# Two attentions in one kernel: output sums added by VectorE alone, and a softmax over eight places cut into short steps

## The chip, the cores and the metric

One Trainium2 chip, one core of it. The metric is the device time of one launch in microseconds (us). Engines are called by the names of the profile: PE (TensorE), with PEld for its weight loads, DVE (VectorE), ACT (ScalarE), POOL (GpSimd), SP (SyncE, which issues nearly all DMAs). Each engine runs its own instructions in order and waits on semaphores for the others.

## The reference

Two attention layers, A and B, on separate inputs of shape 1 x 2048 x 576, with 32 heads of 18 each; their outputs stand side by side. B is plain softmax attention. A looks at eight places only, two positions apart:

```python
W, dil = 8, 2
idx = pos[:, None] - (jnp.arange(W) * dil)[None, :]
mask = idx >= 0
logits = jnp.einsum("bhsd,bhswd->bhsw", q, kg) * scale      # kg, vg: k and v at idx
logits = jnp.where(mask, logits, -1e9)
attn = _softmax(logits, axis=-1)
o = jnp.einsum("bhsw,bhswd->bhsd", attn, vg)
return o.transpose(...).reshape(B, S, D) @ wo
```

## The kernel before, in words

Everything is float32, products split into high and low parts. A first part, up to about 420 us, makes the projections of both layers. Then comes the main loop of 512 steps, which is written out by hand: the program says for every engine in which order it works.

One step is one tile of 128 keys for one block of 512 queries and a group of four heads of B. PE makes four score matmuls (`score`, line 227), each into a bank of the ring "scores" (four PSUM banks); ACT takes the exponential of each (line 233). Beside three or four of the scores PE makes a matmul for the row maxima of a later block (line 162) into the ring "else" (three banks), and DVE reduces each to its maximum (line 169). At the end of the step the exponentials of the step before are weighed with the values (`weigh`, line 700, into the bank `po`).

All other work hangs in an agenda: a function due at step n is called at the end of step n (`due()`), and so stands in the program at that place. The order on each engine follows from that, while an engine may run its instructions earlier than the step, as far as what they wait for allows. Functions due at the same step are called in the order in which they were entered; `later(n, f)` enters f n steps ahead.

- A's attention runs in eight rounds, `local(j)`, j = 0 to 7, one each 54 steps; round j counts its plan from step 10 + 54 j. POOL makes the logits out of nine products (`match`, lines 823 and 827; the sum `lg`, line 830). DVE takes the maximum over the eight places (`most`, line 837, tile `am`), POOL subtracts it (`lower`, 844), ACT takes the exponentials (847), DVE sums them and takes the reciprocal (`total`, 837 and 851, tile `as`), POOL multiplies (`share`, 854) and then makes nine weighted terms (`weighted`, 860 to 863). `upper` and `rest` (867, 872) split the result, `put` and `get` (875, 885, 887) carry it through DRAM into another order. All POOL work of a round takes most of the round's time.
- A's output products, four in each round (two tiles of 128 positions, two halves of 288 columns), are put inside a step between two scores (`sums_of_a`): PE sums the two halves of the contraction in two banks, `one` (of the ring "scores") and `two` (of the ring "else"), beside each other (`beside`, line 979). ACT copies `one`, DVE copies `two` to SBUF, and POOL adds them (line 906).
- When a block of B is done, `finish` copies `po` out and, by `later`, at +7 takes reciprocals of the denominators (731), at +8 and +12 carries them through DRAM to all rows (732, 733), and at +17, +18, +19 POOL scales and splits the result (734, 735, 736). A block ends every 16 steps, so line 734 falls due at steps 33, 49, ..., 193, 209, ...
- The weights of A's output product are loaded and split in five pieces (`load_wo`), due at steps 28, 32, 36, 40 and 44; POOL splits each three steps later (lines 107 and 108).
- `halve` splits the row maxima of B for their way back into the queries (107, 108).

Of the kernel before, what the change touches and what calls it, by code (L numbers as in the profile page):

```python
# [7 lines left out]
F32 = mybir.dt.float32  # L8
F32R = mybir.dt.float32r
BF16 = mybir.dt.bfloat16  # L10
AF = mybir.ActivationFunctionType
ALU = mybir.AluOpType
# [8 lines left out]
W = 8  # L21
# [27 lines left out]
def ap(t, *dims):  # L49

    return bass.AP(tensor=t.tensor, offset=t.offset, ap=[list(t.ap[0])] + [list(d) for d in dims])
# [8 lines left out]
def two_attentions(ctx: ExitStack, tc, xa, wa, woa, xb, wb, wob, c_id, c_sel, out):  # L60
# [56 lines left out]
    def plan(start, pieces):  # L117
        for n, f in pieces:
            agenda[start + n].append(f)
# [100 lines left out]
    def score(g, b, kt, h, also, kind="scores"):  # L220

        assert (g, b) in placed
        qs, ks = sets[g % 3]
        p, r = divmod(h, 2)
        ps = bank(kind)
        at = slice(64 * r, 64 * r + 56)
        nc.tensor.matmul(ps, ks[at, p, 128 * kt : 128 * kt + 128], qs[at, b, p], start=True, stop=True)  # L227
        reduce = maximum(1 - r) if also else None

        counted[0] += 1  # L230
        early = counted[0] % 8 < 6
        e = (e_room if early else work).tile([128, 512], F32, name="e", bufs=6 if early else 2)
        nc.scalar.activation(e, ps, AF.Exp, scale=SCALE)  # L233
        if reduce:
            reduce()
        return e
# [560 lines left out]
    def local(j):  # L797

        st = {}
        p0 = AB * j  # L800

        def arrange(n):
            wide = (HALO if n else 0) + SUB
            load(rows(dparts[j][n][0, 0], (wide, D), (D * wide, 4), (1, wide)),
                 rows(da[D * n, HALO + p0 + SUB - wide :], (HALO + S, D), (SUB, 4), (1, wide)))


        def fetch(nm):
            halo = 0 if nm == "q" else HALO
            n = DH * (halo + SUB)  # L810
            t = st[nm] = work.tile([128, DH, halo + SUB], F32, name="akv" if halo else "aq", bufs=2 if halo else 1)
            load(ap(t, (1, n)), rows(dparts[j]["qkv".index(nm)][0, 0], (n, 128), (1, n)))

        def window(t, c):

            return ap(t[:, 2 * c, HALO:], (HALO + SUB, 2), (-DIL, W), (1, SUB))

        def wide():
            return work.tile([128, 2, W, SUB], F32, name="pr", bufs=2)

        def match(c):
            pr = wide()
            nc.gpsimd.tensor_mul(pr, ap(st["q"][:, 2 * c], (SUB, 2), (0, W), (1, SUB)), window(st["k"], c))  # L823
            if c == 0:
                st["pr"] = pr
            else:
                nc.gpsimd.tensor_add(st["pr"], st["pr"], pr)  # L827
            if c == DH // 2 - 1:
                lg = st["lg"] = work.tile([128, W, SUB], F32, name="lg", bufs=1)
                nc.gpsimd.tensor_add(lg, st["pr"][:, 0], st["pr"][:, 1])  # L830
                if j == 0:
                    for w in range(1, W):
                        nc.gpsimd.memset(lg[:32, w, : DIL * w], MASKED)

        def over_window(op, name):
            t = work.tile([128, SUB], F32, name=name, bufs=1)
            nc.vector.tensor_reduce(t, st["lg"].rearrange("p w i -> p i w"), axis=AX.X, op=op)
            return t

        def most():  # L840
            st["m"] = over_window(ALU.max, "am")

        def lower():
            nc.gpsimd.tensor_sub(st["lg"], st["lg"], ap(st["m"], (0, W), (1, SUB)))

        def exponents():
            nc.scalar.activation(st["lg"], st["lg"], AF.Exp, scale=SCALE)

        def total():
            s = st["s"] = over_window(ALU.add, "as")  # L850
            nc.vector.reciprocal(s, s)

        def share():
            nc.gpsimd.tensor_mul(st["lg"], st["lg"], ap(st["s"], (0, W), (1, SUB)))

        def weighted(c):
            if c == 0:
                st["o"] = work.tile([128, DH, SUB], F32, name="ao", bufs=1)
            at = wide()
            nc.gpsimd.tensor_mul(at, ap(st["lg"], (0, 2), (SUB, W), (1, SUB)), window(st["v"], c))  # L860
            nc.gpsimd.tensor_add(at[:, :, :4], at[:, :, :4], at[:, :, 4:])  # L861
            nc.gpsimd.tensor_add(at[:, :, :2], at[:, :, :2], at[:, :, 2:4])
            nc.gpsimd.tensor_add(st["o"][:, 2 * c : 2 * c + 2], at[:, :, 0], at[:, :, 1])

        def upper():
            hi = work.tile([128, DH, SUB], F32R, name="aohi", bufs=1)
            nc.gpsimd.tensor_copy(hi, st["o"])
            st["parts"] = hi, st["o"].bitcast(F32R)

        def rest():  # L870
            hi, lo = st["parts"]
            nc.gpsimd.tensor_sub(lo, st["o"], hi)

        def put(i):
            load(rows(dao[j, i, 0, 0], (DH * SUB, 128), (1, DH * SUB)),
                 ap(st["parts"][i].bitcast(F32), (1, DH * SUB)))

        def get(n):
            st["x"] = []
            st["n"] = n  # L880
            last = work.tile([128, 128], F32R, name="ahl", bufs=1)
            for i in range(2):
                t = work.tile([128, 4, 128], F32R, name=f"at{i}", bufs=1)
                for s in range(2):
                    load(t.bitcast(F32)[:, :, SUB * s : SUB * s + SUB],
                         dao[j, i, 2 * n + s, :512].rearrange("(c p) n -> p c n", p=128))
                load(last.bitcast(F32)[64 * i : 64 * i + 64].rearrange("p (s n) -> p s n", s=2),
                     rows(dao[j, i, 2 * n, 512], (SUB, 64), (D * SUB, 2), (1, SUB)))
                st["x"].append([t[:, c] for c in range(4)])
            st["x"].append(last)  # L890

        def finished(h):
            inside.append(lambda: sums_of_a(h))

        def sums_of_a(h):
            his, los = zip(*wo["a"])
            w = his[:4], los[:4], his[4], los[4]
            cols = slice(288 * h, 288 * h + 288)
            if h == 0:
                st["y"] = ys["a", j, st["n"]] = work.tile([128, D], F32, name="y", bufs=3)  # L900
            one, two = beside("scores", *(halves(r, 0, w, st["x"], cols, slice(0, 128), True) for r in range(2)))
            y = st["y"][:, cols]
            part = work.tile([128, 288], F32, name="part", bufs=2)
            nc.scalar.activation(y, one, AF.Copy)
            nc.vector.tensor_copy(part, two)  # L905
            nc.gpsimd.tensor_add(y, y, part)  # L906

        plan = {0: lambda: fetch("q"), 1: lambda: fetch("k"), 28: lambda: fetch("v"), 29: most, 30: lower,
                32: exponents, 34: total, 35: share, 58: upper, 59: rest, 66: lambda: put(0), 67: lambda: put(1)}
        for c in range(DH // 2):  # L910
            plan[5 + 5 * c // 2] = lambda c=c: match(c)
            plan[36 + 5 * c // 2] = lambda c=c: weighted(c)
        for n in range(3):
            plan[(-24 if j else -7) + n] = lambda n=n: arrange(n)
        for n in range(2):
            at = 74 + 7 * n
            plan[at] = lambda n=n: get(n)
            plan[at + 4] = lambda: finished(0)
            plan[at + 6] = lambda: finished(1)
            producing.update((A_FROM + GAP * j + at + 5, A_FROM + GAP * j + at + 7))  # L920
            plan[at + 12] = lambda n=n: load(out[p0 + 128 * n : p0 + 128 * n + 128, :D], ys["a", j, n])
        return plan


    olds = defaultdict(list)
# [33 lines left out]


    inside = []

    waiting = []

# [92 lines left out]
    ):  # L1057
        plan(start, [(4 * c, lambda k=k, src=src, ch=ch: load_wo(k, src, *ch)) for c, ch in enumerate(chunks)])
    for j in range(NJ):
        plan(A_FROM + GAP * j, local(j).items())  # L1060
    for g in range(1, NG):
        if g > EARLY:
            plan(STEPS * (g - 2) + 1, [(n, f) for n, f in enumerate(stack_loads(g))])
# [35 lines left out]
    while step < ALL:  # L1099
        n, kt = divmod(step, NT)  # L1100
        g, b = divmod(n, NB)
        places = positions(min(4 if behind() > 0 else 3, total - sum(given)))
        es = []
        for h in range(4):

            if inside and h == (3 if 3 in places else 2):
                inside.pop(0)()
            es.append(score(g, b, kt, h, h in places))
        while waiting:
            waiting.pop(0)()  # L1110
        if ready:
            weigh(*ready.pop(0))
        ready.append((g, b, kt, es))
        due()
        if waiting:
            waiting.pop(0)()
        step += 1
# [30 lines left out]
```

## Time and profile before

| | |
|---|---|
| median of 3 runs | 1677.24 us (1673.43 to 1678.26) |
| the profiled execution, its own time | 1677.95 us |
| its span in the profile | 1676.2 us |
| mean granted PE clock | 0.998 |
| busy: PE, DVE, ACT, POOL | 1664.2, 1410.6, 1223.3, 998.6 us |

The span runs from the first instruction to the last; the execution's own time has 1.75 us more around it. Rows of a timeline give the start in us from the span's start, the duration, engine, line of the kernel, operation, result and operands, shapes and count, and in brackets the idle time of the engine before it, with what ended it. Rows of a group give, behind the shapes, the count, then total busy us, mean ns of one, and the idle time before them.

### The profile page before, as it was taken

Reading aid. Unit: us, or ns where it says so; the run is one execution under the profiler, and the core shown is the slowest. Engines: PE = TensorE matmul, PEld = TensorE weight load, DVE = VectorE, ACT = ScalarE, POOL = GpSimd, SP = SyncE. Lnnn points to the kernel's source line nnn. Section 1 sums busy time; section 2 is a strip of 40 time slices with the busy share of each in tenths; the row PEclk is TensorE's granted clock in tenths of the full one; section 3 lists DMA queues with packets and bytes.
Section 4 is the critical chain, followed back from the end, with each engine's and each line's share of the span. In section 5 each row is a group of like instructions: output and inputs, shape, how many; then the busy total and the mean of one; then the engine's idle time right before and its main releaser. Section 6 shows DMA issues by size and latency. Waiting matters only on the chain.

```text
span 1676.2 us, 33705 instructions
## 1 busy us (share of the span) xinstructions
PE 1664.2 (99%) x12994; PEld 922.9 (55%) x12994; DVE 1410.6 (84%) x2318; ACT 1223.3 (73%) x2420; POOL 998.6 (60%) x842
## 2 busy tenths in 40 slices
PE   9999999999999999999999999999999999999998
PEld 7998888887433444344444344444444344344765
DVE  5199999999889989889889988889888989888433
ACT  6423521211999988988988987998988988988444
POOL 2306732100286996986984996986995997812010
PEclk9999999999999999999999999999999999999999
DMA  8938944421624536165247128227526222134101
GB/s 246 242 108 220 264 141 135 139 90 66 94 82 62 142 99 107 59 155 115 66 107 156 64 84 181 70 63 134 132 64 131 76 76 77 35 98 170 57 30 58
DMA packets 186082, 188.37 MB, mean 112 GB/s; under 512 B 114832, under 2 KB 129936, under 8 KB 184192
## 3 DMA queue, kind: packets, MB, share of 16 engines
q1 hardware_dynamic: 181056, 174.66, 40.1%
q0 software_dynamic: 4032, 10.63, 3.1%
q8 instruction: 102, 1.67, 0.4%
q10 hardware_dynamic: 832, 0.92, 0.2%
q14 instruction: 60, 0.49, 0.1%
HBM read 113.30 MB, written 88.12 MB: 120 GB/s over the span
## 4 chain that ended last, share of the span: by engine, by line
PE 89%; POOL 6%; SPq 2%; DVE 1%; DMA 1%; issue 1%; ACT 0%; POOLq 0%; ACTq 0%; DVEq 0%
PE po L700 27%; PE bank L227 21%; PE bank L320 14%; PE bank L162 14%; PE bank L979 7%; PE bank L257 4%; SPq L146 1%; POOL pr L823 1%; POOL pr L860 1%; POOL pr L827 1%; DVE mx L169 1%; POOL pr L861 1%; DMA rec<-drec 1%; PE bank L958 1%; PE bank L181 0%
## 5 line engine op out<-in xcount | busy, mean ns | idle before, releaser
L169 DVE TENSOR_REDUCE mx<-bank 128x1 f32<-128x512 f32 x2048 | 1294.4, 685 | 154.1 <-PE bank L162 132.0
L233 ACT ACTIVATE e<-bank 128x512 f32<-128x512 f32 x2048 | 1060.4, 610 | 108.6 <-PE bank L227 57.1
L162 PE MATMUL bank<-ks,qs 54*128 54x512 f32 x2048 | 757.6, 424 | 5.0 <-DVE mx L169 2.7
L227 PE MATMUL bank<-qs,ks 56*128 56x512 f32 x2048 | 582.9, 425 | 0.0
L227 PEld LDWEIGHTS bank<-qs,ks 56*128 56x128 f32 x2048 | 327.2, 186 | 430.7 <-ACT e L233 403.1
L700 PE MATMUL po<-e,v 128*19 128x512 f32 x4096 | 541.0, 600 | 0.0
L162 PEld LDWEIGHTS bank<-ks,qs 54*128 54x128 f32 x2048 | 342.8, 185 | 34.2 <-DVE mx L169 16.8
L823 POOL TENSOR_TENSOR pr<-aq,akv 128x1024 f32<-128x1024 f32 x72 | 157.9, 2197 | 24.6 <-PE po L700 22.3
L700 PEld LDWEIGHTS po<-e,v 128*19 128x19 f32 x4096 | 69.8, 97 | 181.7 <-issue 170.7
L860 POOL TENSOR_TENSOR pr<-lg,akv 128x1024 f32<-128x1024 f32 x72 | 158.1, 2195 | 0.3
L827 POOL TENSOR_TENSOR pr<-pr 128x1024 f32<-128x1024 f32 x64 | 152.4, 2382 | 5.0
L651 ACT ACTIVATE ohi<-bank 128x512 f32<-128x512 f32 (+1 forms) x56 | 30.4, 595 | 155.2 <-issue 124.4
L320 PE MATMUL bank<-xlo,ahi 64*128 64x512 f32 (+1 forms) x448 | 121.8, 391 | 0.1
L320 PE MATMUL bank<-xhi,alo 64*128 64x512 f32 (+1 forms) x448 | 118.6, 390 | 0.0
L320 PE MATMUL bank<-xhi,ahi 64*128 64x512 f32 (+1 forms) x448 | 115.2, 392 | 0.0
L906 POOL TENSOR_TENSOR y<-y,part 128x288 f32<-128x288 f32 x32 | 25.6, 799 | 117.8 <-DVE part L905 102.4
L861 POOL TENSOR_TENSOR pr<-pr 128x512 f32<-128x512 f32 x72 | 92.4, 1283 | 5.6
L461 POOL TENSOR_TENSOR olo<-olo,ohi 128x512 fp32r<-128x512 f32 x36 | 46.2, 1298 | 68.3 <-ACT ohi L460 67.1
L368 POOL TENSOR_TENSOR alo<-raw,ahi 128x512 fp32r<-128x512 f32 (+1 forms) x14 | 17.6, 1254 | 115.1 <-ACT ahi L367 90.6
L320 PEld LDWEIGHTS bank<-xlo,ahi 64*128 64x128 f32 (+1 forms) x448 | 68.1, 182 | 9.4 <-POOL xlo L368 0.5
L320 PEld LDWEIGHTS bank<-xhi,alo 64*128 64x128 f32 (+1 forms) x448 | 65.4, 182 | 9.1
L979 PE MATMUL bank<-wohi,at 64*128 64x288 f32 x512 | 68.9, 301 | 0.0
(194 smaller groups left out, 1845.4 us busy)
## 6 DMA issues: line engine op xcount, KB each, us to landing
do<-n SPq DMA_DIRECT2D x28, 512.0 KB
da<-ohi SPq DMA_DIRECT2D x52, 256.0 KB
dpart<-da SPq DMA_DIRECT2D x16, 702.0 KB
akv<-dpart SPq DMA_DIRECT2D x16, 702.0 KB
out<-y SPq DMA_DIRECT2D x32, 288.0 KB
qs<-dqk SPq DMA_DIRECT2D x30, 288.0 KB
ks<-dqk SPq DMA_DIRECT2D x30, 288.0 KB
at<-dao SPq DMA_DIRECT2D x64, 128.0 KB
```

What stands on the lines that cost most here:

```text
L162: nc.tensor.matmul(ps, qs[at, b, p, 128 * t : 128 * t + 128], ks[at, p, 512 * k : 512 * k + 512], start=True, stop=True)
L169: nc.vector.tensor_reduce(mx[:, r, p, t, k : k + 1], ps, axis=AX.X, op=ALU.max)
L227: nc.tensor.matmul(ps, ks[at, p, 128 * kt : 128 * kt + 128], qs[at, b, p], start=True, stop=True)
L233: nc.scalar.activation(e, ps, AF.Exp, scale=SCALE)
L257: nc.tensor.matmul(ps, a, b, start=c == i == 0, stop=c == 4 and i == 1)
L320: nc.tensor.matmul(ps, a, b, start=start, stop=stop)
L700: nc.tensor.matmul(po[32 * i : 32 * i + 19], vs[g][:, kt, 19 * i : 19 * i + 19], es[i], start=kt == 0, stop=kt == NT - 1)
L823: nc.gpsimd.tensor_mul(pr, ap(st["q"][:, 2 * c], (SUB, 2), (0, W), (1, SUB)), window(st["k"], c))
L827: nc.gpsimd.tensor_add(st["pr"], st["pr"], pr)
L860: nc.gpsimd.tensor_mul(at, ap(st["lg"], (0, 2), (SUB, W), (1, SUB)), window(st["v"], c))
L861: nc.gpsimd.tensor_add(at[:, :, :4], at[:, :, :4], at[:, :, 4:])
L979: nc.tensor.matmul(ps, a, b, start=start, stop=stop)
```

## The change

In the output products ACT copies `two` to SBUF, and DVE adds `one` to it from PSUM, in place. That addition is not called at once but entered in a new list, `outside`, which is emptied after the step's four scores (and so after the reductions beside them); POOL's addition is gone.

In A's softmax the reduction over eight places becomes three tensor_tensor steps on DVE, halving the places each time (8 to 4, 4 to 2, 2 to 1), for the maxima and for the sums alike; the reciprocal is taken in two halves of 32 columns. In the round's plan `most` falls on steps 29, 30, 30 (was 29), `lower` on 31 (30), the exponentials on 33 (32), `total` on 35, 36, 36 (34), the two halves of the reciprocal on 36 and 37, `share` on 38 (35), the nine `weighted` from 39 on (36), `upper` on 61 (58), `rest` on 62 (59), `put` on 67 and 68 (66, 67). The matches, fetches, gets and output products keep their steps.

```diff
-        def over_window(op, name):
-            t = work.tile([128, SUB], F32, name=name, bufs=1)
-            nc.vector.tensor_reduce(t, st["lg"].rearrange("p w i -> p i w"), axis=AX.X, op=op)
-            return t
-
-        def most():
-            st["m"] = over_window(ALU.max, "am")
+        def over_window(op, name, n):
+
+            if n == 0:
+                st[name] = work.tile([128, W // 2, SUB], F32, name=name, bufs=1)
+            t, half = st[name], W >> n + 1
+            src = st["lg"] if n == 0 else t
+            nc.vector.tensor_tensor(t[:, :half], src[:, :half], src[:, half : 2 * half], op=op)
+
+        def most(n):
+            over_window(ALU.max, "am", n)
...
-        def total():
-            s = st["s"] = over_window(ALU.add, "as")
-            nc.vector.reciprocal(s, s)
+        def total(n):
+            over_window(ALU.add, "as", n)
+
+        def inverse(n):
+            half = st["as"][:, 0, SUB // 2 * n : SUB // 2 * n + SUB // 2]
+            nc.vector.reciprocal(half, half)
...
-            part = work.tile([128, 288], F32, name="part", bufs=2)
-            nc.scalar.activation(y, one, AF.Copy)
-            nc.vector.tensor_copy(part, two)
-            nc.gpsimd.tensor_add(y, y, part)
-
-        plan = {0: lambda: fetch("q"), 1: lambda: fetch("k"), 28: lambda: fetch("v"), 29: most, 30: lower,
-                32: exponents, 34: total, 35: share, 58: upper, 59: rest, 66: lambda: put(0), 67: lambda: put(1)}
+            nc.scalar.activation(y, two, AF.Copy)
+            outside.append(lambda: nc.vector.tensor_add(y, one, y))
+
+        plan = {0: lambda: fetch("q"), 1: lambda: fetch("k"), 28: lambda: fetch("v"), 31: lower,
+                33: exponents, 38: share, 61: upper, 62: rest, 67: lambda: put(0), 68: lambda: put(1)}
+
+        short = [(at, lambda f=f, n=n: f(n)) for f, ats in ((most, (29, 30, 30)), (total, (35, 36, 36)), (inverse, (36, 37)))
+                 for n, at in enumerate(ats)]
         for c in range(DH // 2):
             plan[5 + 5 * c // 2] = lambda c=c: match(c)
-            plan[36 + 5 * c // 2] = lambda c=c: weighted(c)
+            plan[39 + 5 * c // 2] = lambda c=c: weighted(c)
...
             es.append(score(g, b, kt, h, h in places))
+        while outside:
+            outside.pop(0)()
         while waiting:
```

More of the change, by code (lines that the diff above doesn't have):

```diff
@@ L833, in match @@
                         nc.gpsimd.memset(lg[:32, w, : DIL * w], MASKED)
-        def over_window(op, name):
-            t = work.tile([128, SUB], F32, name=name, bufs=1)
-            nc.vector.tensor_reduce(t, st["lg"].rearrange("p w i -> p i w"), axis=AX.X, op=op)
-            return t
-        def most():
-            st["m"] = over_window(ALU.max, "am")
+        def over_window(op, name, n):
[6 more added lines that the diff above has]
+            over_window(ALU.max, "am", n)
         def lower():
-            nc.gpsimd.tensor_sub(st["lg"], st["lg"], ap(st["m"], (0, W), (1, SUB)))
+            nc.gpsimd.tensor_sub(st["lg"], st["lg"], ap(st["am"], (0, W), (1, SUB)))
         def exponents():
             nc.scalar.activation(st["lg"], st["lg"], AF.Exp, scale=SCALE)
-        def total():
-            s = st["s"] = over_window(ALU.add, "as")
-            nc.vector.reciprocal(s, s)
+        def total(n):
[3 more added lines that the diff above has]
+            nc.vector.reciprocal(half, half)
         def share():
-            nc.gpsimd.tensor_mul(st["lg"], st["lg"], ap(st["s"], (0, W), (1, SUB)))
+            nc.gpsimd.tensor_mul(st["lg"], st["lg"], ap(st["as"], (0, W), (1, SUB)))
         def weighted(c):
@@ L921, in local @@
             plan[at + 12] = lambda n=n: load(out[p0 + 128 * n : p0 + 128 * n + 128, :D], ys["a", j, n])
-        return plan
+        return [*plan.items(), *short]
     olds = defaultdict(list)
@@ L961, in two_attentions @@
     inside = []
+    outside = []
     waiting = []
@@ L1059, in two_attentions @@
     for j in range(NJ):
-        plan(A_FROM + GAP * j, local(j).items())
+        plan(A_FROM + GAP * j, local(j))
     for g in range(1, NG):
```

## The prediction

> **What bounds the kernel now.** I read the page first, then the groups of instructions by line, the waits, the chain, and the timelines of single engines in a few windows.
>
> ```profile
> span 1676.2 us, 33705 instructions
> ...
> PE 1664.2 (99%) x12994; PEld 922.9 (55%) x12994; DVE 1410.6 (84%) x2318; ACT 1223.3 (73%) x2420; POOL 998.6 (60%) x842
> ```
>
> TensorE sets the time; only what keeps it waiting is worth anything. A step of the main loop (four score matmuls, three maximum matmuls, the weighing at line 700) begins each weighing one period after the last. Two stretches of TensorE's timeline, then VectorE's in a normal step:
>
> ```profile
> 1261.30 1.05 PE L700 MATMUL po<-e,v 128*19 128x512 f32 x8
> 1263.41 1.05 PE L700 MATMUL po<-e,v 128*19 128x512 f32 x8
> 1266.09 1.05 PE L700 MATMUL po<-e,v 128*19 128x512 f32 x8
> ...
> 1153.61 1.05 PE L700 MATMUL po<-e,v 128*19 128x512 f32 x8
> 1156.30 1.05 PE L700 MATMUL po<-e,v 128*19 128x512 f32 x8
> ```
>
> ```profile
> 1004.93 1.89 DVE L169 TENSOR_REDUCE mx<-bank 128x1 f32<-128x512 f32 x3 [0.23 <-PE bank L162]
> ```
>
> A normal period is 2.11 us (1263.41 - 1261.30). Two are long: 2.68 us, after round 6's maxima, and 2.69 us, after round 5's sums. In a step VectorE works 1.89 us and rests 0.23; a long operation between holds up its reductions, these hold three banks, and TensorE waits for a bank. That is what the split into short steps can remove: 0.57 us for the maxima, 0.58 for the sums, in each of eight rounds.
>
> There is a much dearer form of the same wait, once in the run, when VectorE stands at the maxima and GpSimd has not yet made the logits:
>
> ```profile
> 1009.66 1.03 DVE L837 TENSOR_REDUCE am<-lg 128x64 f32<-128x512 f32 x1 [2.84 <-POOL lg L830]
> ```
>
> ```profile
> 1007.62 1.05 PE L700 MATMUL po<-e,v 128*19 128x512 f32 x8
> ...
> 1011.35 0.79 PE L162 MATMUL bank<-ks,qs 54*128 54x512 f32 x1 [2.24 <-DVE mx L169]
> ...
> 1013.69 1.91 PE L700 MATMUL po<-e,v 128*19 128x512 f32 x8
> ```
>
> ```profile
> 1008.60:1017.20 8.60, 6.36 (x28) 3.32 (x26) 5.42 (x9) 4.08 (x8) 4.28 (x4) 0.63 1.12 145
> ```
>
> The last row is a table by stretch: its length, the busy time of each engine, then the granted clock. VectorE is blocked for 3.87 us (2.84 + 1.03). The period is 6.07 us (1013.69 - 1007.62), 3.96 over normal; and afterwards the granted clock is 0.63 over 8.6 us, weighing takes 1.91 instead of 1.05, so I put the whole loss at 5.7 us: the 1.7 is an estimate for the next, slowed period, between the 0.86 of its weighing and the 3.2 (8.6 x 0.37) of the whole window. [...]
>
> **The change, part by part.** The groups that carry the prices:
>
> ```profile
> L169 DVE TENSOR_REDUCE mx<-bank 128x1 f32<-128x512 f32 x2048 | 1294.4, 685 | 154.1 <-PE bank L162 132.0 <-PE bank L227 10.9 <-PE bank L320 1.1
> ...
> L906 POOL TENSOR_TENSOR y<-y,part 128x288 f32<-128x288 f32 x32 | 25.6, 799 | 117.8 <-DVE part L905 102.4 <-ACT y L904 13.1 <-ACT e L233 2.3
> ...
> L999 DVE TENSOR_TENSOR y<-bank,y 128x288 f32<-128x288 f32 x24 | 11.0, 458 | 2.5
> ...
> L837 DVE TENSOR_REDUCE as<-lg 128x64 f32<-128x512 f32 x8 | 8.5, 1062 | 0.0
> L837 DVE TENSOR_REDUCE am<-lg 128x64 f32<-128x512 f32 x8 | 8.4, 1054 | 2.8 <-POOL lg L830 2.8
> ...
> L731 DVE RECIPROCAL den<-den 128x16 f32<-128x16 f32 x29 | 7.0, 243 | 0.0
> ...
> L851 DVE RECIPROCAL as<-as 128x64 f32<-128x64 f32 x8 | 4.4, 553 | 0.3
> ```
>
> *Short steps.* No row shows tensor_tensor at these sizes. From 685 ns for 512 elements and 458 for 288 (1.01 ns an element, 0.17 fixed) I estimate 0.43 us for 256, 0.30 for 128 and 0.23 for 64; a half reciprocal, between 243 ns for 16 and 553 for 64, 0.35. Maxima: 0.43 in one step, 0.53 in the next, instead of 1.05 at once. Sums and reciprocal: 0.43, then 0.88 (0.30 + 0.23 + 0.35), then 0.35, instead of 1.62 (1.06 + 0.55). VectorE's work hardly shrinks; it is spread. What then remains of the 1.15 us a round? The maxima row says that 1.05 us in one place loses 0.57, so 0.48 is absorbed; by that measure 0.43 and 0.53 lose almost nothing in the maxima, but 0.88 loses about 0.4 and the 0.35 behind it 0.1 more, and if backlogs add up up to 1.1 us. The sums row says that 1.62 loses only 0.58, so 1.04 is absorbed, and nothing would remain. I take 0.4 a round, nearer to the sums row because the pieces concerned are its own. Removed: six maxima stalls of 0.57 (rounds 1 and 4 are treated below) and eight of 0.58, 8.1 us; left, 8 x 0.4 = 3.2. Sum -4.9 us.
>
> *Output products.* ScalarE copies the other bank, at the same place and price. VectorE's copy (0.45 us, first row below) becomes an addition (458 ns): the same, nothing. But it moves behind the step's last reduction and holds the bank of the scores ring that ScalarE used to free. The bank is wanted in the next step:
>
> ```profile
> 1250.41 0.45 DVE L905 COPY part<-bank 128x288 f32<-128x288 f32 x1
> 1250.78 0.68 DVE L169 TENSOR_REDUCE mx<-bank 128x1 f32<-128x512 f32 x1
> ```
>
> ```profile
> 1251.86 0.39 PE L227 MATMUL bank<-qs,ks 56*128 56x512 f32 x1
> ```
>
> Order swapped, the reduction ends at about 1251.1 and the addition at 1251.56, 0.3 us before the score matmul that reuses the bank. What is queued behind the addition is the next step's reductions, and they would have stood behind the copy too. Below: nothing is gained, since the maximum ring's bank, now freed earlier, is not what TensorE waits for. Above: one late VectorE operation of 0.2 us in each of 32, 6 us. I take one in eight, 0.8 us.
>
> GpSimd loses 32 x 0.8 = 25.6 us of work and 117.8 us of standing in order for it. None of this is on TensorE's path by itself; it counts only through the logits' readiness, next.
>
> *The shifted plan.* A's lower, exponents, share, weighted terms and puts move by 1, 1, 3, 3 and 1 steps. GpSimd works in order, so what matters is what now stands ahead of share. Finishing steps of B and weight splits fall due at fixed steps, and two of them wait for a DMA. Round 0: share moves from step 45 to 48, and the split of A's last weight piece is due at step 47:
>
> ```profile
> 521.35 1.28 POOL L854 TENSOR_TENSOR lg<-lg,as 128x512 f32<-128x512 f32 x1 [2.90 <-DVE as L851]
> ...
> 529.61 0.67 POOL L107 CAST wohi<-y 128x576 fp32r<-128x576 f32 x1 [2.00 <-DMA y<-woa]
> ...
> 531.73 2.21 POOL L860 TENSOR_TENSOR pr<-lg,akv 128x1024 f32<-128x1024 f32 x1
> ```
>
> Before, share and the first weighted term filled the time to 527.6 (529.61 - 2.00). Now GpSimd idles until the DMA lands at 529.5, splits, and does these 6.26 us (527.61 - 521.35) from 531.7 on. Behind that it is busy without a rest until round 1's logits:
>
> ```profile
> 626.11 1.28 POOL L830 TENSOR_TENSOR lg<-pr 128x512 f32<-128x512 f32 x1
> ```
>
> ```profile
> 629.51 1.05 DVE L837 TENSOR_REDUCE am<-lg 128x64 f32<-128x512 f32 x1
> ```
>
> They were ready at 627.39, 2.1 us before they were wanted. With +6.26 and one addition of 0.8 less they come at 632.85, 3.3 us late. VectorE is blocked 3.3 + 0.43 = 3.8 us, as long as in the stall shown above, so the same 5.7 us instead of 0.57: +5.1.
>
> Round 3: share moves from step 207 to 210, and the scaling of B's outputs (line 734), due at 209, now stands ahead of it. It waited for the DMA of the reciprocals, held up in the SP queue by loads of keys:
>
> ```profile
> 899.54 2.19 POOL L860 TENSOR_TENSOR pr<-lg,akv 128x1024 f32<-128x1024 f32 x1
> ...
> 903.98 0.46 POOL L863 TENSOR_TENSOR ao<-pr 128x128 f32<-128x128 f32 x1
> 914.08 1.29 POOL L734 TENSOR_TENSOR o<-o,rec 128x512 f32<-128x512 f32 x1 [9.64 <-DMA rec<-drec]
> ```
>
> Share (1.28, as in round 0) and the first term (903.98 + 0.46 - 899.54 = 4.9) move behind the 9.64 us wait: 6.2, less one addition, 5.4 us more for round 4's logits, which are the late ones. VectorE's first piece is 0.6 shorter: +4.7.
>
> The puts (one step later) wait on SP for upper and rest, which now stand behind one or two match products; SP is held a few us in rounds 0 and 3. Queued there are gets due six steps later, 12.7 us, which covers it; uncovered, the output products would wait for what is left of that hold.
>
> *The lock.* The new steps read two tensors of SBUF while GpSimd may be reading:
>
> ```profile
> 20.45 1.37 DVE L368 TENSOR_TENSOR xlo<-raw,xhi 128x512 fp32r<-128x512 f32 x1 [0.98 <-ACT xhi L367]
> ```
>
> ```profile
> 19.98 1.29 POOL L461 TENSOR_TENSOR olo<-olo,ohi 128x512 fp32r<-128x512 f32 x1 [19.04 <-ACT ohi L460]
> ```
>
> Such a VectorE step took 1.37 us and ended 0.55 after GpSimd's. In most rounds GpSimd waits for the very result, so it is idle; only finishing work of rounds 6 and 7 overlaps. Between 0 and 4 x 0.9 us I take 0.7. [...]
>
> **Sum**, against the profiled run's own 1677.95 us (0.7 above the median 1677.24): -4.9 + 0.8 + 5.1 + 4.7 + 0.7 = +6.4, so 1684.4 us.
>
> **Rivals.** (a) The two DMAs land earlier than in this one execution, or the stalls are absorbed: then -4.9 + 1.5 = -3.4, 1674.5, and with nothing left of the stalls (-8.1) 1671.3. For: both are single waits of 2.0 and 9.64 us. Against: GpSimd has no slack behind them. Chance 0.24. (b) Only one of the two comes late: 1679.5. Chance 0.17. (c) More rounds are late, share being 5 us later everywhere (three periods of 2.11, less 1.3 that one half reciprocal is shorter than reduction and reciprocal). The tightest is round 7, whose logits led by 2.5 us:
>
> ```profile
> 1384.39 1.28 POOL L830 TENSOR_TENSOR lg<-pr 128x512 f32<-128x512 f32 x1
> ```
>
> ```profile
> 1388.19 1.07 DVE L837 TENSOR_REDUCE am<-lg 128x64 f32<-128x512 f32 x1
> ```
>
> Of these, about 3 return as three finishing operations of B, of line 734's 1.29 us or less, go ahead of share, and 0.8 with the addition. Where 1 or 2 us fail to return, it costs 2 to 4: 1688. Chance 0.10. (d) The lock blocks each first piece in all rounds, 8 x 0.9 = 7.2 us, which decides from the point where GpSimd still has finishing work at that step: 1691.6. Chance 0.04. My forecast keeps 0.45.
>
> **Numbers.** 0.3% (about what a measurement of this kernel can tell from no change) is 5.0 us: 1672.2 to 1682.3. Forecast, (c) and (d) lie above for the most part, less some of the forecast's lower half: slower 0.52; (b), most of (a) and that half: same 0.35; the rest of (a): faster 0.13. The range runs from 1673 (most of (a)) to 1690.
>
> **What would show it.** Right: POOL's split of A's weights ahead of share in round 0, line 734 ahead of it in round 3; waits of VectorE's first maxima piece for lg in rounds 1 and 4, of about 3 and 8 us; normal 2.1 us periods after the maxima in rounds 2, 3, 5. Wrong: no wait for lg over 3 us; or periods still of 2.7 us with pieces of 0.4 us; or score weights waiting for VectorE's addition in most of the 32 products.

## The result, and the profile after

The changed kernel takes 1682.59 us (median of 8 runs, 1680.95 to 1688.06), the kernel before 1676.97 on the same chips (8 runs, 1673.43 to 1678.32). The ratio is 1.0038, with a 95% interval of 1.0026 to 1.0051: slower by 5.6 us. The profiled execution of the changed kernel took 1681.28 us, at a mean granted clock of 0.994 (0.998 before); it is 3.3 us over the profiled execution of before. Three executions in the experiments below took far longer than all others (2213, 3044 and 8662 us) and count in no ratio.

The page of the changed kernel, its span, the busy times and the shares of the chain that ended last:

```profile
span 1679.5 us, 33707 instructions
...
PE 1661.5 (99%) x12994; PEld 924.5 (55%) x12994; DVE 1410.0 (84%) x2358; ACT 1223.5 (73%) x2420; POOL 973.8 (58%) x810
...
PE 87%; POOL 8%; DVE 2%; DMA 1%; issue 1%; ACT 1%; SPq 0%; POOLq 0%; ACTq 0%; DVEq 0%
```

VectorE has as much work as before (1410.0 against 1410.6 us), GpSimd 24.8 less, and yet GpSimd holds 8% of the chain, about 134 us (6% before). Two rows of the waits and two of VectorE's timeline show where VectorE waits for it, and where it waits itself:

```profile
DVE am L841 <- POOL lg L830: 11.2, 2, 7.9
...
POOL wohi L107 <- DMA y<-woa: 10.6, 1, 10.6
```

```profile
631.18 0.42 DVE L841 TENSOR_TENSOR am<-lg 128x256 f32<-128x256 f32 x1 [3.23 <-POOL lg L830]
...
1015.55 0.43 DVE L841 TENSOR_TENSOR am<-lg 128x256 f32<-128x256 f32 x1 [7.93 <-POOL lg L830]
```

Before there was one wait of VectorE for the logits, of 2.8 us; now there are two, in rounds 1 and 4. GpSimd's timeline shows what stands ahead of `share` in the rounds before them:

```profile
528.14 0.66 POOL L107 CAST wohi<-y 128x576 fp32r<-128x576 f32 x1 [10.58 <-DMA y<-woa]
528.89 1.43 POOL L108 TENSOR_TENSOR wolo<-y,wohi 128x576 fp32r<-128x576 f32 x1
530.26 1.28 POOL L860 TENSOR_TENSOR lg<-lg,as 128x512 f32<-128x512 f32 x1
...
915.20 1.29 POOL L734 TENSOR_TENSOR o<-o,rec 128x512 f32<-128x512 f32 x1 [16.00 <-ACT e L233]
916.44 1.28 POOL L860 TENSOR_TENSOR lg<-lg,as 128x512 f32<-128x512 f32 x1
```

The second wait carries ACT's name, not the DMA's. The operation is the one that waited for the DMA of the reciprocals before, and that DMA was issued at 907.35 in this execution, 7.9 us ahead of line 734 (905.21 before, 8.9 us ahead); I read it as the same wait; in the kernel with the softmax part alone, below, the profile names the DMA in this row (16.51 us).

What TensorE sees of it, in its weighings: round 1, round 4, and last a round in which the new steps do what they are for (the first piece of round 6's maxima runs at 1266.60):

```profile
628.76 1.05 PE L700 MATMUL po<-e,v 128*19 128x512 f32 x8
634.61 1.91 PE L700 MATMUL po<-e,v 128*19 128x512 f32 x8
641.30 1.05 PE L700 MATMUL po<-e,v 128*19 128x512 f32 x8
...
1008.41 1.05 PE L700 MATMUL po<-e,v 128*19 128x512 f32 x8
1018.97 1.91 PE L700 MATMUL po<-e,v 128*19 128x512 f32 x8
1024.73 1.05 PE L700 MATMUL po<-e,v 128*19 128x512 f32 x8
...
1265.36 1.05 PE L700 MATMUL po<-e,v 128*19 128x512 f32 x8
1267.47 1.05 PE L700 MATMUL po<-e,v 128*19 128x512 f32 x8
1269.58 1.05 PE L700 MATMUL po<-e,v 128*19 128x512 f32 x8
```

Rounds 1 and 4 in the kernel before, round 4 from its second weighing on:

```profile
630.39 1.05 PE L700 MATMUL po<-e,v 128*19 128x512 f32 x8
633.06 1.05 PE L700 MATMUL po<-e,v 128*19 128x512 f32 x8
637.35 1.05 PE L700 MATMUL po<-e,v 128*19 128x512 f32 x8
...
1013.69 1.91 PE L700 MATMUL po<-e,v 128*19 128x512 f32 x8
1019.70 1.05 PE L700 MATMUL po<-e,v 128*19 128x512 f32 x8
```

Two periods of 2.11 us stand behind round 6's maxima, where one of 2.68 stood before. But round 1 takes 5.85 + 6.69 (2.67 + 4.29 before), and round 4 takes 10.56 + 5.76 (6.07 + 6.01 before).

### The profile page after: what moved, and what is told of

Same layout as the page of the kernel before. It is cut to its first block, busy times and chain, and to the rows that moved or that the text cites. A ratio compares the mean times of both kernels' runs of the same rounds, so it can differ in the third digit from the quotient of the medians.

```text
span 1679.5 us, 33707 instructions
## 1 busy us (share of the span) xinstructions
PE 1661.5 (99%) x12994; PEld 924.5 (55%) x12994; DVE 1410.0 (84%) x2358; ACT 1223.5 (73%) x2420; POOL 973.8 (58%) x810
## 4 chain that ended last, share of the span: by engine, by line
PE 87%; POOL 8%; DVE 2%; DMA 1%; issue 1%; ACT 1%; SPq 0%; POOLq 0%; ACTq 0%; DVEq 0%
PE po L700 26%; PE bank L227 21%; PE bank L320 14%; PE bank L162 14%; PE bank L988 7%; PE bank L257 4%; POOL pr L823 2%; POOL pr L827 2%; DVE mx L169 1%; POOL pr L866 1%; POOL pr L867 1%; PE bank L965 1%; DMA y<-woa 0%; POOL pr L868 0%; PE bank L181 0%
## 5 line engine op out<-in xcount | busy, mean ns | idle before, releaser
L107 POOL CAST mh<-mt 16x128 fp32r<-16x128 f32 x32 | 9.0, 280 | 120.3 <-DVE mt L183 120.3
L734 POOL TENSOR_TENSOR o<-o,rec 128x512 f32<-128x512 f32 x29 | 37.3, 1285 | 57.2 <-ACT e L233 56.7
```

## The experiments

**Theory:** the short steps do remove VectorE's stalls (some 7 us), and two GpSimd operations that wait for a DMA, now ahead of `share` in rounds 0 and 3, give back about 10. **Rival 1:** the output products' addition on VectorE costs TensorE a bank. **Rival 2:** GpSimd's later order makes the logits late in many rounds. **Rival 3:** the cutting of the steps does the good and their spread over steps is not needed.

### One wait moved: the last weight piece of A

```diff
-        later(3, lambda: split_on(nc.gpsimd, hi[:n], lo[:n], raw[:n]))
+        later(5 if k == "a" and len(wo[k]) == 5 else 3, lambda: split_on(nc.gpsimd, hi[:n], lo[:n], raw[:n]))
```

> Changed kernel, but the split of the last piece of A's output weights is called two steps later (step 49, behind share at 48). Theory (GpSimd idles for that piece's DMA ahead of share, so round 1's logits come late): GpSimd no longer waits ahead of share in round 0, VectorE's wait of 3.3 us for lg in round 1 is gone, the two periods 5.85 and 6.69 us become 2.12 and 4.28; 6.1 us less than the changed kernel, about 1676.5 us, level with before. Rival 1 (the loss comes from VectorE's addition that holds a bank of scores): no change, 1682.6. Rival 2 (the loss comes from short steps that stand still while GpSimd reads): no change in round 1's wait for lg; under 1 us.

1678.1 us, ratio to the kernel before 1.0008 (1.0000 to 1.0017). TensorE's weighings in round 1:

```profile
628.81 1.05 PE L700 MATMUL po<-e,v 128*19 128x512 f32 x8
631.94 1.05 PE L700 MATMUL po<-e,v 128*19 128x512 f32 x8
636.21 1.05 PE L700 MATMUL po<-e,v 128*19 128x512 f32 x8
```

The two periods are 3.13 + 4.27 instead of 5.85 + 6.69, so 5.14 us come back: the wait for the weights was the cause in round 1. The time falls by 4.5 us only, not the 6.1 expected. One part of that is in round 4, which this edit doesn't touch and which stalls for 12.45 + 5.12 in this profile, 1.25 us more than in the changed kernel. The other is a rest of 1.0 us over a normal period in round 1, which I had not expected. GpSimd's and VectorE's rows give the sum of it:

```profile
526.05 1.28 POOL L860 TENSOR_TENSOR lg<-lg,as 128x512 f32<-128x512 f32 x1 [8.41 <-ACT e L233]
...
627.69 1.29 POOL L830 TENSOR_TENSOR lg<-pr 128x512 f32<-128x512 f32 x1
```

```profile
629.01 0.42 DVE L841 TENSOR_TENSOR am<-lg 128x256 f32<-128x256 f32 x1 [0.99 <-POOL lg L830]
```

`share` starts at 526.05, 4.70 later than before (521.35). Of this 2.00 returns, since the split's wait is gone, and 1.1 since GpSimd has less to do (one addition of 0.8 fewer ahead of the logits; where the other 0.3 comes from is not shown): the logits end at 628.98, 1.6 later than before (627.39). And VectorE, which no longer stalls in round 0, wants them at 628.02, 1.5 earlier than before (629.51). Together 3.1, against a lead of 2.1: 1.0 late. The last experiment but one puts this to the test.

### The other wait moved, and both

```diff
-            later(at, f)
+            later(at + 2 if (g, b) == (2, 3) and 16 < at < 20 else at, f)
```

> Changed kernel, but the three finishing operations of one block of B (lines 734 to 736, the block that ends at step 191) are called two steps later, behind share and the first weighted term of round 3. Theory: GpSimd waits for the reciprocals with share and one term already done, round 4's logits come about 6 us earlier, VectorE's wait of 7.9 us for them shrinks to about 2, the period of 10.55 us to 4 or 5; 6 us less than the changed kernel, about 1676.5 us. Rival 1 and rival 2: no change, 1682.6.

1677.92 us, ratio 1.0002 (0.9993 to 1.0011). Round 4 falls from 10.56 + 5.76 to 7.08 + 5.94, less than expected (4 or 5 for the first), because GpSimd still waits at line 734, for 5.87 us, now behind `share` and the first weighted term only. Round 1, which this edit doesn't touch, takes 6.59 + 6.95 in this profile, 1.0 us more than in the changed kernel.

> Both of these edits together. Theory: the gains add, 12 us less than the changed kernel, about 1670.5 us, and 6 us less than before: what remains is the gain of the short steps, 0.8 to 1.4 us in each round. Rivals: 1682.6, no gain.

1671.78 us, ratio 0.9968 (0.9956 to 0.9980): with both moved, the change is faster than the kernel before. Round 4 still takes 5.82 + 6.64, and GpSimd's timeline names the DMA this time:

```profile
911.29 1.28 POOL L734 TENSOR_TENSOR o<-o,rec 128x512 f32<-128x512 f32 x1 [4.61 <-DMA rec<-drec]
```

So two steps are too few. The next version moves line 734 (and 735 and 736) by five steps, and the split by six: it falls due nine steps after its load instead of three.

> Changed kernel, with the last split of A's output weights six steps later (step 53) and the finishing operations of the block that ends at step 191 five steps later (214 to 216). Theory: GpSimd waits nowhere ahead of the logits of rounds 1 and 4, VectorE waits for lg in no round, all periods at the maxima are 2.12 us; against the kernel with both edits by two steps (1671.8) 6.0 us less in round 4 and 0.9 in round 1: about 1665 us, 12 less than before. Rival (a rest of round 4's stall has another cause, the loads of keys): round 4 keeps 5 us or more, 1670 us.

1666.61 us, ratio 0.9938 (0.9925 to 0.9951). The stall of round 4 is gone in TensorE's weighings: 2.12 us after the maxima, then an ordinary product period of 4.35.

```profile
1003.37 1.05 PE L700 MATMUL po<-e,v 128*19 128x512 f32 x8
1005.49 1.05 PE L700 MATMUL po<-e,v 128*19 128x512 f32 x8
1009.84 1.05 PE L700 MATMUL po<-e,v 128*19 128x512 f32 x8
```

The further move of the split changed nothing in round 1 (3.18 + 4.27): its rest has nothing to do with that wait. The time stays 1.6 us over the 1665 expected, and this rest is 1.1 of it.

### Each half of the change alone

The output products' part alone, in the kernel before:

```diff
-            nc.scalar.activation(y, one, AF.Copy)
-            nc.vector.tensor_copy(part, two)
-            nc.gpsimd.tensor_add(y, y, part)
+            nc.scalar.activation(y, two, AF.Copy)
+            outside.append(lambda: nc.vector.tensor_add(y, one, y))
...
```

> Kernel before with the first part of the change alone: ScalarE copies the other bank, VectorE adds the first from PSUM behind the step's reductions, GpSimd adds nothing; A's softmax and its plan are those of before. Theory: 32 periods with an output product stay at 4.3 to 4.4 us; round 4's logits come 0.8 us earlier (one GpSimd addition less ahead of them), so 1 to 2 us are gained there: about 1675.5 us. Rival 1 (the addition holds the scores' bank too long): those periods grow by 0.2 us each, 1682 to 1683 us.

1678.72 us, ratio 1.0007 (0.9999 to 1.0016). No period with an output product grew (4.27 to 4.42 us in both kernels, apart from one of 4.69, before 4.68, and the one in round 4's stall), so rival 1 falls as it was put. The addition isn't quite free, though: the period at A's sums, two steps behind a product, is 2.80 to 2.83 us in rounds 1, 2, 4, 5 and 7, where it was 2.68 to 2.70. And the gain that I had expected from GpSimd's 25.6 us less isn't there: the wait for the DMA of the reciprocals was 10.6 us in its profile (9.6 before), and round 4 stalled for 6.01 + 5.78. Work taken from an engine that then waits longer for the same DMA brought nothing here.

The softmax part alone, with the old copies and GpSimd's addition (the tiles `am` and `as` share one buffer here, for space):

```diff
-            nc.scalar.activation(y, two, AF.Copy)
-            outside.append(lambda: nc.vector.tensor_add(y, one, y))
+            part = work.tile([128, 288], F32, name="part", bufs=2)
+            nc.scalar.activation(y, one, AF.Copy)
+            nc.vector.tensor_copy(part, two)
+            nc.gpsimd.tensor_add(y, y, part)
...
```

> Kernel with the second part of the change alone: short steps and the new plan, but the output products' sums are copied by VectorE and added by GpSimd as before (the maxima and the sums share one tile, to make room). Theory: GpSimd has 3.2 us more work in each round and waits in order for VectorE's copies ahead of the logits (3.7, 2.3, 4.9 us in rounds of before), so logits are late in more rounds than 1 and 4: round 7, which led by 0.5 us in the changed kernel, and round 6 or 3; at least 4 waits of VectorE for lg, 1686 to 1694 us. Rival (GpSimd's additions are off the path and count nothing): as the changed kernel, 1682.6.

1685.41 us, ratio 1.0055 (1.0041 to 1.0069), against 1.0038 (1.0026 to 1.0051) for the whole change; the intervals overlap. The waits of VectorE for the logits:

```profile
DVE am L841 <- POOL lg L830: 14.5, 2, 9.3
```

Two waits again, each longer (rounds 1 and 4: 8.40 + 5.44 and 12.45 + 5.77), not four or more as rival 2 would have it. The slowdown belongs to the softmax part.

### Cut, but not spread

The pieces stay, and all stand at the steps of the kernel before:

```diff
-        short = [(at, lambda f=f, n=n: f(n)) for f, ats in ((most, (29, 30, 30)), (total, (35, 36, 36)), (inverse, (36, 37)))
+        short = [(at, lambda f=f, n=n: f(n)) for f, ats in ((most, (29, 29, 29)), (total, (34, 34, 34)), (inverse, (34, 34)))
```

(and with them, not shown, the rest of the plan: `share` at 35 and so on)

> Changed kernel, but with the plan of before: the three steps of the maxima stand together at step 29, the three of the sums and the two half reciprocals together at 34, share at 35. Theory (what gains is that the work lies in several steps, not that it is cut): 0.97 us and 1.7 us stand in one place as before, the long periods stay at about 2.6 and 2.7 us, share is not late, so rounds 1 and 4 are as before: 1676 to 1678 us. Rival (the cut itself gains): periods of 2.1 to 2.3 us without the late share, 1669 to 1671 us.

1675.35 us, ratio 0.9991 (0.9982 to 1.0000). The weighings around round 6's maxima:

```profile
1259.53 1.05 PE L700 MATMUL po<-e,v 128*19 128x512 f32 x8
1262.14 1.05 PE L700 MATMUL po<-e,v 128*19 128x512 f32 x8
```

2.61 us, where the whole reduction gave 2.68 and the spread pieces 2.11; at the sums 2.75 to 2.78 in most rounds. Rival 3 falls: spreading removes the stall, cutting alone does not. It is still 2.4 us under the kernel before (1677.78 on that chip), by an interval that just touches no difference. In the profiles (spans of 1672.9 and 1676.2) the gain is in round 4, which takes 4.41 + 4.28 instead of 6.07 + 6.01: the logits are 1.7 us late instead of 2.8, and behind the shorter stall, 1.07 us of TensorE's idling, the granted clock stayed at 1.00 (last section). Why they are less late isn't settled. GpSimd has its additions no more, and its wait for the reciprocals was 9.2 us instead of 9.6; in the kernel with the output products' part alone the additions were gone too, the wait was 10.6, and the logits came 3.3 us late.

### The lock

On top of the version with both waits moved further, lines 734 to 736 of another block are moved by two steps, so that line 734 isn't running on GpSimd when round 7's maxima are made:

```diff
-            later(at + 5 if (g, b) == (2, 3) and 16 < at < 20 else at, f)
+            later(at + {(2, 3): 5, (6, 0): 2}.get((g, b), 0) if 16 < at < 20 else at, f)
```

> The same, and the finishing operations of the block that ends at step 399 two steps later (419 to 421), so that GpSimd's line 734 does not stand beside the second and third maxima step of round 7. Theory (these two steps, 1.56 us for the pair instead of 0.51, stood still while GpSimd read): the pair takes 0.5 us, the period of 4.94 us in round 7 becomes 4.28, 0.66 us less than the kernel without this edit. Rival (they are slow by themselves there): no change.

1666.19 us, ratio 0.9936 (0.9922 to 0.9950), 0.4 under the version without it, which these intervals don't part. The rows can. First VectorE and GpSimd in round 7 of the changed kernel, then VectorE in this one:

```profile
1393.64 1.56 DVE L841 TENSOR_TENSOR am<-am 128x128 f32<-128x128 f32 x2
```

```profile
1393.16 1.28 POOL L734 TENSOR_TENSOR o<-o,rec 128x512 f32<-128x512 f32 x1
```

```profile
1378.66 0.54 DVE L841 TENSOR_TENSOR am<-am 128x128 f32<-128x128 f32 x2
```

The pair of small pieces takes 1.56 us while GpSimd multiplies two tiles of SBUF, and 0.54 when GpSimd does so later; the next product period is 4.94 us in the one and 4.27 in the other. In the version without the edit, the direct comparison, the pair took 1.55 us and the period was 5.03. The same shows elsewhere: in that version GpSimd's line 734 also met the first piece of round 5's maxima, which took 0.91 us instead of 0.42. What holds the pieces up beside line 734 is not shown.

### The rest of round 1

Round 0's whole softmax chain one step earlier, on top of that:

```diff
-        short = [(at, lambda f=f, n=n: f(n)) for f, ats in ((most, (29, 30, 30)), (total, (35, 36, 36)), (inverse, (36, 37)))
+        short = [(at - (j == 0), lambda f=f, n=n: f(n)) for f, ats in ((most, (29, 30, 30)), (total, (35, 36, 36)), (inverse, (36, 37)))
...
+        if j == 0:
+            plan.update({30: lower, 32: exponents, 37: share})
...
```

> On top of the version with both GpSimd waits moved and the lock avoided (1666.19 us), round 0's softmax chain (maxima, subtraction, exponentials, sums, reciprocals, share) is taken one step earlier, as in the kernel before for the maxima. What is to be told apart is the 1.0 us by which round 1's logits still come late. Theory A: GpSimd's work from round 0's share to round 1's logits is a fixed chain of about 103 us, and share stands one step too late in it, since VectorE no longer stalls and wants the logits sooner. Then share starts about 2.1 us earlier (524.0 instead of 526.1), the wait of the first maxima piece for the logits in round 1 goes, the period at round 1's maxima falls from 3.2 to 2.1, and the time is 1665.1 (1664.3 to 1666.0). Theory B: GpSimd's nine products of round 1 are paced by something else (their data from DRAM, or their steps), and the chain has rest in it: then the logits do not move against the maxima, the period stays at 3.1 to 3.2, and the time stays at 1666.2.

1666.18 us, ratio 0.9931 (0.9917 to 0.9945). Its profile is read from a second run of the same kernel.

> The same kernel as e9_round0_earlier, for its profile: that run's profiled execution was disturbed (3043 us), and its time, 1666.18, did not move against 1666.19. If theory B holds, the first maxima step of round 1 is still 3.1 to 3.2 us and the wait for the logits 1.0. If theory A holds, that step is 2.1 us and the logits come ahead of VectorE, and about 1 us must have been given back elsewhere: in round 0, where the exponentials, the reciprocals or the products now stand one step earlier, or in round 1's next period.

1665.56 us (3 runs), ratio 0.9929 (0.9907 to 0.9952). GpSimd's `share` and logits, then TensorE's weighings in round 1:

```profile
523.67 1.28 POOL L860 TENSOR_TENSOR lg<-lg,as 128x512 f32<-128x512 f32 x1 [6.30 <-ACT e L233]
...
625.38 1.29 POOL L830 TENSOR_TENSOR lg<-pr 128x512 f32<-128x512 f32 x1
```

```profile
628.77 1.05 PE L700 MATMUL po<-e,v 128*19 128x512 f32 x8
630.90 1.05 PE L700 MATMUL po<-e,v 128*19 128x512 f32 x8
635.18 1.05 PE L700 MATMUL po<-e,v 128*19 128x512 f32 x8
```

`share` starts 2.4 us earlier, the logits follow by the same, and the period falls from 3.2 to 2.13, with 4.28 behind it. So the rest in round 1 was `share` standing one step too late for a GpSimd without slack. In this profile half of that microsecond is given back in round 5: the first piece of the maxima meets GpSimd's line 734 there and takes 1.06 us instead of 0.42, and the period is 2.67 instead of 2.11. In time the edit is worth less than these runs resolve: the spans of the two profiles are 1663.1 and 1664.4, the medians 1666.18 and 1665.56 against 1666.19.

### What the kernel before would gain by the same cure

The kernel before with line 734 to 736 of block (2, 3) five steps later, and nothing else:

```diff
-            later(at, f)
+            later(at + 5 if (g, b) == (2, 3) and 16 < at < 20 else at, f)
```

> The kernel before, with one thing moved: the scaling and splitting of one block of B's outputs (lines 734 to 736, block (2,3)) falls due 5 steps later. It tells how much of the gain of the improved versions is the change's own, and how much is the cure of a stall that the kernel before has too. Theory A (the stall at round 4's maxima in the kernel before comes from GpSimd's wait of 9.6 us for the DMA of the reciprocals ahead of round 3's weighted terms): the wait shrinks below 5 us, the first maxima step of round 4 goes from 6.07 to about 2.7 and the next from 6.01 to 4.3, 5.1 us less than the kernel before: 1672.3 (1671 to 1674), so that the change with its two waits moved and the lock avoided (1666.2) is itself worth about 6. Theory B (round 4's logits are late because GpSimd has too much work there, whatever it waits for): the period stays above 5 and the time within 1.5 of the kernel before, about 1677.

1672.99 us, ratio 0.9977 (0.9966 to 0.9987). Its stall in round 4 is gone:

```profile
1007.25 1.05 PE L700 MATMUL po<-e,v 128*19 128x512 f32 x8
1009.91 1.06 PE L700 MATMUL po<-e,v 128*19 128x512 f32 x8
1014.19 1.05 PE L700 MATMUL po<-e,v 128*19 128x512 f32 x8
```

2.66 + 4.28 instead of 6.07 + 6.01: the kernel before had one late round by this DMA, and the maxima's own stall of 0.55 is left. Run on the same chip, this kernel is 6.8 us slower than the change with its waits, the lock and the late `share` out of the way (1666.18). That is what the change is worth with what hides it cured on both sides, and it is the size of what the short steps removed.

## Why the prediction was right, point by point

The time came 1.8 us under the forecast (1684.4), and by the mechanism that the forecast named. Term by term, read from TensorE's periods in the two profiled executions:

| step of the prediction | predicted | measured |
|---|---|---|
| stalls removed by the short steps, less what is left | -4.9 | -6.9 |
| the addition holds a bank | +0.8 | 0 |
| round 1 late | +5.1 | +5.6 |
| round 4 later still | +4.7 | +4.2 |
| the lock | +0.7 | +0.7, all in round 7 |
| sum | +6.4 | +3.6 |

The spans of the two profiles differ by 3.3 (another 0.2 is gained ahead of the main loop), the medians by 5.6. The changed kernel's profiled execution was one of its shorter ones (1681.28 of 1680.95 to 1688.06). A likely reason is that the time GpSimd stands at line 734 depends on when a DMA lands, which differs from profile to profile (last section); for executions of one and the same kernel no run shows it. So part of the good agreement of 1684.4 with the median is that a sum against one profile came out too high, and the profiled execution below its kind.

*Short steps.* Mis-sized, by 2.0 us. The larger part is in what was removed: the prediction took 0.58 us, read in round 5, for the sums of each round, but in the kernel before these periods were 2.97, 3.43 and 3.16 us in rounds 0, 3 and 6, which is 0.85, 1.31 and 1.04 over a normal one. The rest is in what remains, for which I took 0.4 us a round. After the maxima nothing is left (2.12 us in rounds 2, 3, 5 and 6, as the prediction's last part asked), after the sums 0.25 in most rounds (periods of 2.27 and 2.22). The rows of the new pieces, from the groups by form (count, then busy us and mean ns, then idle time before):

```profile
L910 DVE TENSOR_TENSOR y<-bank,y 128x288 f32<-128x288 f32 x32 | 14.3, 447 | 0.0
L857 DVE RECIPROCAL as<-as 128x32 f32<-128x32 f32 x16 | 5.6, 348 | 0.3
L841 DVE TENSOR_TENSOR am<-lg 128x256 f32<-128x256 f32 x8 | 3.3, 417 | 11.2 <-POOL lg L830 11.2
...
L841 DVE TENSOR_TENSOR as<-as 128x128 f32<-128x128 f32 x8 | 2.5, 312 | 0.0
...
L841 DVE TENSOR_TENSOR as<-as 128x64 f32<-128x64 f32 x8 | 1.8, 225 | 0.3
```

Against the estimates (0.43 for 256 elements, 0.30 for 128, 0.23 for 64, 0.35 for half a reciprocal) the prices held. I had doubted whether the backlog of one piece is worked off when the next comes; the 0.25 that remains in most rounds lies between nothing, which the sums row gave, and the 0.4 that I took.

*The addition.* The bound from below was the right end: no product period grew, in the whole change or alone; what it lengthens, by 0.1 us, is the period at the uncut sums (in the kernel with the output products' part alone), which the prediction doesn't have.

*Round 1.* The place, the wait and the price hold. Logits were to be 3.3 us late and were 3.23. Both had moved by 1.6 us (627.95 wanted instead of 629.51, since round 0 stalls less; the weights' DMA let GpSimd go on at 528.1 instead of 529.5), so the agreement to 0.1 is partly luck. The period behind the stall cost 2.4 us where I had estimated 1.7 from round 4.

*Round 4.* VectorE was to wait about 8 us and waited 7.93. The terms of the working give +4.8, not +4.7 (1.28 + 4.90 - 0.80 - 0.60). Measured are 4.5 in the stalled period (10.56 against 6.07), less 0.25 since the slowed period behind it was shorter.

*The lock.* No run shows 0.9 us for a step, which was my estimate; the runs showed 1.02 us for a pair of steps (1.56 against 0.54) and 0.67 in the period (4.94 against 4.27). That 0.7 came out as 0.7 is luck: the bounds were 0 and 3.6, and it was one pair of pieces in one round.

*The rivals.* (a) and (b) did not happen by themselves, but the runs made them: with one of the two waits gone the time is 1678.1 or 1677.9 (rival (b) said 1679.5), with both largely gone 1671.8 (rival (a): 1671.3 to 1674.5). (c), more rounds late, did not come even with GpSimd's additions left in; its margin was thinner than it looked, since round 1 was still 1.0 us late without any wait. (d), the lock in all rounds, came in one.

## What to carry to other kernels

Here the cutting of a long operation on VectorE (84% busy) took the stall away only with the pieces spread over steps: the period at round 6's maxima was 2.11 us with the pieces spread, 2.61 with the same pieces side by side and 2.68 with the operation whole. Where an engine works without rest from one hand-over to the next, as GpSimd does from round 0's `share` to round 1's logits (95.2 of the 98.8 us from 530.2 to 629.0 in the changed kernel), look at what a shifted order puts ahead of the first of that work, above all at operations that wait for a DMA: here two of them cost 10 us (5.6 and 4.2) and hid a gain of about 7. And once a stall is gone, look again at when the engine that stalled wants its next input: VectorE wanted round 1's logits 1.5 us sooner (628.02 instead of 629.51), so that the lead of 2.1 us read from the old trace was too long.

## What the runs showed of the hardware

In three stalls the granted clock went down to 0.50, and the longest idling did not make the work behind it the slowest. Tables by stretch, set to the ends of the slow stretch, after TensorE's idling of 2.02 us in round 1 and of 6.73 in round 4 of the changed kernel, and of 2.67 in round 4 of the kernel with the output products' part alone (length, busy times of PE, PEld, DVE, ACT and POOL, granted clock, DMA share, GB/s):

```profile
633.26:640.09 6.83, 6.83 (x37) 4.07 (x37) 4.22 (x9) 3.13 (x6) 4.43 (x4) 0.50 0.90 158
1012.14:1022.38 10.24, 5.75 (x23) 3.02 (x25) 5.15 (x11) 2.53 (x5) 7.16 (x6) 0.50 1.06 138
...
1013.80:1017.21 3.41, 3.41 (x19) 1.66 (x13) 1.90 (x4) 1.55 (x4) 1.86 (x2) 0.50 1.38 98
```

The clock was at 0.50 for 6.83, 10.24 and 3.41 us, but in the second case the stretch began (1012.14) while TensorE was still idle (until 1016.63), so that it worked for 5.75 us of it. The period behind the stall cost 2.4, 1.5 and 1.5 us over an ordinary one (1.7 in the kernel before, after 2.24 us of idling; in the kernels with one of the two waits moved, 2.7 after 2.95 us and 0.8 after 8.63). So in these stalls the price did not grow with the idling, and it lay between 0.8 and 2.7 us. In the kernel that is cut but not spread, TensorE was not busy for 1.07 us (8.00 - 6.93) at round 4's stall, and the clock stayed at 1.00:

```profile
1004.00:1012.00 8.00, 6.93 (x41) 2.80 (x45) 6.02 (x13) 7.02 (x14) 6.59 (x6) 1.00 0.80 206
```

So 1.07 us of idling left the clock at 1.00 in one profile, and 2.02 us stood ahead of a clock of 0.50 in another; that the length of one idle stretch decides is not shown. From the kernel that is cut but not spread to the kernel before (2.24 us of idling), round 4 goes from 8.69 us (4.41 + 4.28) to 12.08 (6.07 + 6.01), 3.4 us more, for logits that come 1.2 us later.

And the time from the issue of round 3's DMA of the reciprocals to line 734, where GpSimd stood waiting for it, varies by profile: 7.9 us in the changed kernel, 8.9 before, 9.5 with the softmax part alone, 10.4 with the split moved, 10.7 with the output products' part alone. What stands behind such a wait may vary with it: the changed kernel's eight runs spread over 7.1 us (3.6 without the longest), the five of the version with both waits moved further over 2.5. That the DMA is the cause of this spread is not shown.
